# Blocks aligned with batches, their leftovers as a ninth block, and attention between groups of six matmuls

## The chip, the cores and the metric

The kernel runs on one core of a Trainium2 chip. The metric is the device time of one execution in microseconds (us); the time before is the median of three runs. Engines are named as in the profile: PE is TensorE's matmul, PEld its weight load, DVE VectorE, ACT ScalarE, POOL GpSimd, SP SyncE, which here issues every DMA.

## What is computed

```python
# q, k, v: (8 batches, 8 heads, 576 tokens, 64)
scores = q @ k.T / 8
mask_local   = (0 <= rel) & (rel < 32)                  # heads 0 to 3
mask_strided = (0 <= rel) & (pos_k % 32 == pos_q % 32)  # heads 4 to 7
x = softmax(masked scores) @ v        # -> (8, 576, 512), heads side by side
u = x + V.T @ (U.T @ x)               # over tokens; U: 576 x 32, V: 32 x 576
out = u + relu(u @ w_ch1) @ w_ch2     # w_ch1: 512 x 2048, w_ch2: 2048 x 512
```

So each of the 4608 tokens goes through attention inside its batch, a mixing of low rank over the tokens of its batch, and an MLP.

## The kernel before

**The MLP** works on u transposed: features on the partitions, tokens along the free axis, in blocks of `TB` = 512 tokens. 8 x 576 tokens make `NB` = 9 blocks. Every operand is kept as two parts, a rounded one and the remainder (`uh` and `ul`, `gh` and `gl`, two parts of each weight), and a product takes three matmuls. `gemm1(n, fc)` (L413) makes 128 hidden features of block n from four feature chunks: 12 matmuls of 128x128 by 128x512 into `ph`, then ACT (L417) and DVE (L418) make `gh` and `gl`. `gemm2(n, fc)` (L428) adds their part to four accumulators of 512 tokens, again 12 matmuls. There are `NFC` = 16 such chunks fc in a block, and gemm2 runs `LAG` = 2 chunks behind gemm1. `finish(n)` (L431) adds `ul` on DVE (L435) and `uh` on POOL (L436) and stores four tiles `o`. Weights come as 64-bit floats and are converted on chip in 32 chunks (`convert`, ACT L82 and L110, DVE L84 to L87, POOL L111); some in the prefix, the rest in block 0.

**Attention of batch b** is made while block b - 1 runs through the MLP, and that of batch 0 in a prefix (`first_attention`). A pair of heads is a generator (`attention_pair`): loads of kT, qT and vt; scores on PE (mask L143, products L149); maximum and difference on DVE (L157, L158); exponential on ACT (L161); transposes on PE (L170) and a copy on ACT (L173); outputs on PE (L181); normalising on DVE into `x_loc` or `x_str` (L195, L200). Local heads (pairs 0 and 1) always go this way. Strided heads (pairs 2 and 3) do so in batches 0 and 1 (`NSP` = 2). For batches 2 to 7 `strided_heads(b)` makes them with products on POOL (L260, L286) and sums on DVE (L262, L288); their q, k, later v, and their output `o_str[b]` all lie in the one tile `st`, loaded by three DMAs of 576 KB, and at the end ACT copies them into `x_str` (L303, L307).

**Mixing.** `mix_t(b, half)` multiplies x by U on PE (L318, L322) and ends on ACT and DVE in the small tile `tst` (L326 to L335); half 0 is the local heads, half 1 the strided ones. `u_part(b, dc, phase)` then makes u for feature chunk dc: for local heads transposes of x (L389) and a matmul with V (L393) on top of them in PSUM; for strided heads of late batches a matmul (L380) and a DVE add (L382) onto `o_str`. `split` writes `uh` on ACT (L349) and `ul` on DVE or POOL (L350).

**Two phases.** A batch has 576 tokens and a block 512, so batch b fills block b from column 64b on with its first 512 - 64b tokens, and its last 64(b + 1) tokens begin block b + 1. Phase 1 is done in block b - 1, phase 2 in block b (`stretch`). For batches 0 and 1 the strided half of phase 2 waits in the tile `stash`.

**Order.** `stages_of(n)` lists generators with a first and a last chunk; after each gemm1 a `Stage` takes as many steps as put it at its due place. In block n (for b = n + 1, from 2 on) phase 2 of batch n has chunks 2 and 3, the strided heads 4 to 12, the pairs one after the other and local mixing 4 to 10, strided mixing and phase 1 of batch b 13 and 14. The code is then laid out by a scheduler that lists each engine's instructions by priority (the order of the code) and by its own simulated time, and gives out buffers, so neighbours on an engine are not always neighbours in the code.

**Buffers that are shared.** Outside the prefix all small stages (scores, transposes, outputs, mixing, u) take turns in one PSUM tile `px` (`psx2`). In SBUF the tag `att` has `ATT_BUFS` = 7 buffers for kT, qT, s_sb, PT, ta, cv, the strided products tmp and the o tiles. vt and st have one buffer, uh and ul two.

Of the kernel before, what the change touches and what calls it, by code (L numbers as in the profile page):

```python
# [32 lines left out]
def fused_kernel(ctx, tc, lqk, lv, eqk, ev, sqkv, U, V, wts, masks, eye, out):  # L33
# [4 lines left out]
    ap_ = ctx.enter_context(tc.tile_pool(name="ap", bufs=1))  # L38
    ps_acc = ctx.enter_context(tc.tile_pool(name="ps_acc", bufs=2, space=bass.MemoryType.PSUM))
# [77 lines left out]
    stash = ap_.tile([128, 2, 128], F32, name="stash", tag="s_st")  # L117
# [196 lines left out]
    def mix_t(b, half):  # L314
# [9 lines left out]
        yield  # L324
# [4 lines left out]
        yield  # L329
# [6 lines left out]
        yield  # L336

    uT = {}
# [6 lines left out]
    def split(n, dc, cols, src, engine, order=None):  # L345
        uh, ul = (z[:, dc, cols] for z in block_u(n))
        if order is not None:
            uh, ul = uh.rearrange("p (i r) -> p r i", r=32), ul.rearrange("p (i r) -> p r i", r=32)
        nc.scalar.copy(out=uh, in_=src)  # L349
        engine.tensor_tensor(out=ul, in0=src, in1=uh.bitcast(F32), op=ALU.subtract)  # L350

    def stretch(b, phase):
        s0 = TB - 64 * b
        return (b, 0, s0, 64 * b) if phase == 1 else (b + 1, s0, S, 0)

    def u_part(b, dc, phase):
        n, lo, hi, col = stretch(b, phase)
        cols = slice(col, col + hi - lo)
        tst = tsts[b][:, 128 * dc:128 * dc + 128]
        strided = dc >= 2  # L360
        if strided and b < NSP:
            if phase == 2:
                split(n, dc, cols, stash[:, dc - 2, 0:hi - lo], nc.gpsimd)
                return
            px = psx2().rearrange("p a x -> p (a x)")
            for t in range(5):
                w = 128 if t < 4 else 64
                xin = x_str[0:w, t, 128 * dc - 256:128 * dc - 128]
                nc.tensor.matmul(px[:, 128 * t:128 * t + w], xin, ident[0:w, 0:w], is_transpose=True,
                                 start=t in (0, 4), stop=False, skip_group_check=True)  # L370
            nc.tensor.matmul(px[:, 0:512], tst, Vp[:, 0:512], start=False, stop=True, skip_group_check=True)
            nc.tensor.matmul(px[:, 512:576], tst, Vp[:, 512:576], start=False, stop=True, skip_group_check=True)
            src = px[:, 0:S].rearrange("p (r i) -> p r i", i=NCH)
            split(n, dc, cols, src[:, :, 0:hi // 32], nc.vector, True)
            w = S - hi
            nc.scalar.copy(out=stash[:, dc - 2, 0:w].rearrange("p (i r) -> p r i", r=32), in_=src[:, :, hi // 32:NCH])
            return
        if strided:
            px = psx2()[:, 0, 0:hi - lo]
            nc.tensor.matmul(px, tst, Vst[:, lo:hi], start=True, stop=True)  # L380
            src = o_str[b][:, dc - 2, lo:hi]
            nc.vector.tensor_tensor(out=src, in0=px, in1=src, op=ALU.add)  # L382
            split(n, dc, cols, src, nc.gpsimd)
            return
        px = psx2().rearrange("p a x -> p (a x)")
        base, top = lo // 128 * 128, min(S, (hi + 127) // 128 * 128)
        for s in range(base, top, 128):
            w = min(128, top - s)
            nc.tensor.matmul(px[:, s - base:s - base + w], x_loc[0:w, s // 128, 128 * dc:128 * dc + 128], ident[0:w, 0:w],  # L389
                             is_transpose=True, start=(s - base) % 512 == 0, stop=False, skip_group_check=True)  # L390
        for s in range(base, top, 512):
            w = min(512, top - s)
            nc.tensor.matmul(px[:, s - base:s - base + w], tst, Vst[:, s:s + w], start=False, stop=True,  # L393
                             skip_group_check=True)
        split(n, dc, cols, px[:, lo - base:hi - base], nc.vector)

    def u_parts(b, phase, dcs=range(NDC)):
        for dc in dcs:
            u_part(b, dc, phase)
            yield  # L400
# [5 lines left out]
    def gemm1(n, fc):  # L406
# [4 lines left out]
        for dc in range(NDC):  # L411
            for i, (part, ut) in enumerate(((0, uh), (0, ul), (1, uh))):
                nc.tensor.matmul(ph, w_parts[0, g, dc][:, part, fs], ut[:, dc, :],  # L413
                                 start=(dc == 0 and i == 0), stop=(dc == NDC - 1 and i == 2))
        gh = gp.tile([128, TB], F32R, name="gh")
# [3 lines left out]
        return gh, gl  # L419

    def gemm2(n, fc, gh, gl):
# [3 lines left out]
        for m in range(NDC):  # L425
            ms = slice(128 * m, 128 * m + 128)
            for i, (gt, part) in enumerate(((gh, 0), (gl, 0), (gh, 1))):
                nc.tensor.matmul(accs[n][m // 2][:, m % 2], w_parts[1, g, f][:, part, ms], gt,  # L428
                                 start=(fc == 0 and i == 0), stop=(fc == NFC - 1 and i == 2))

    def finish(n):  # L431
        uh, ul = uT[n]
        for m in range(NDC):
            o = att([128, TB], "o")
            nc.vector.tensor_tensor(out=o, in0=accs[n][m // 2][:, m % 2], in1=ul[:, m].bitcast(F32), op=ALU.add)  # L435
            nc.gpsimd.tensor_tensor(out=o, in0=o, in1=uh[:, m].bitcast(F32), op=ALU.add)  # L436
            dma(out=out[m][:, TB * n:TB * n + TB], in_=o)
# [14 lines left out]
    def first_attention():  # L452
# [32 lines left out]
        yield from mix_t(0, 1)  # L485
        yield from mix_t(0, 0)
        for _ in u_parts(0, 1):
            convert(wl["conv"] + 1)
            yield

    def pairs_of(b):
        if b < NSP:
            yield from run_staggered([attention_pair(b, pr) for pr in PAIR_ORDER], 6)
            yield from mix_t(b, 1)
        else:
            yield from attention_pair(b, 0)
            yield from attention_pair(b, 1)
        yield from mix_t(b, 0)

    def rest_of(b):  # L500
        if b >= NSP:
            yield from mix_t(b, 1)
        yield from u_parts(b, 1)

    for _ in first_attention():
        pass
# [7 lines left out]
    class Stage:  # L514
        def __init__(self, gen, start, end, total):
            self.gen, self.start, self.end, self.total, self.done = gen, start, end, total, 0

        def run(self, step):
            if self.gen is None or step < self.start:
                return  # L520
            want = 10 ** 6 if step >= self.end else self.total * (step + 1 - self.start) // (self.end + 1 - self.start)
            while self.done < want:
                self.done += 1
                if next(self.gen, "end") == "end":
                    self.gen = None
                    return

    def stages_of(n):
        b = n + 1
        if b == 1:  # L530
            return [Stage(u_parts(0, 2), 0, 0, 4), Stage(pairs_of(1), 1, 12, 36), Stage(rest_of(1), 13, 14, 4)]
        found = [Stage(u_parts(n, 2), LAG, LAG + 1, 4)] if n < B else []
        if b < B:
            found += [Stage(strided_heads(b), LAG + 2, 12, 82), Stage(pairs_of(b), LAG + 2, 10, 24), Stage(rest_of(b), 13, 14, 7)]
        return found
# [101 lines left out]
```

## Time and profile before

| what | us |
|---|---|
| median of 3 runs (986.08 to 988.97) | 986.51 |
| profiled execution | 990.67 |
| its span in the profile | 988.9 |
| granted clock over the span | 0.958 |
| PE busy / PEld busy | 927.8 / 732.8 |
| DVE / ACT / POOL busy | 541.1 / 252.4 / 414.9 |

Busy times are sums of instruction durations, with overlaps taken once. A matmul's duration contains its fill and drain, so a stream of matmuls looks busy throughout and its price is the distance from start to start. An idle time carries the instruction that released the engine. The granted clock is a share of TensorE's full clock. The views are the page (totals, 40 slices, chain, groups), the stretches (busy time by engine between two times), the timeline, the waits, and the chain of waits.

### The profile page before, as it was taken

How to read it: one execution, taken by the hardware profiler on the slowest of the kernel's cores; microseconds unless marked ns; L12 is line 12 of the kernel's file. 1: busy time of each engine (PE TensorE's matmuls, PEld its weight loads, DVE VectorE, ACT ScalarE, POOL GpSimd, SP SyncE). 2: the span in 40 equal slices, each digit the busy share in tenths (PEclk: the TensorE clock that was granted, in tenths of full speed). 3: DMA queues.
4: the chain of work that ended last, by engine and by line, in shares of the span. 5: the costliest groups of instructions: out<-in, count | busy, mean ns of one | idle time of the engine just before them, and what ended most of it. 6: DMA issues, size and time to landing. Idle time of an engine off the chain costs nothing.

```text
span 988.9 us, 16540 instructions
## 1 busy us (share of the span) xinstructions
PE 927.8 (94%) x6906; PEld 732.8 (74%) x6906; DVE 541.1 (55%) x942; ACT 252.4 (26%) x519; POOL 414.9 (42%) x433
## 2 busy tenths in 40 slices
PE   4689978999999999999999989999899989999996
PEld 2467756687778777888688868887688868888885
DVE  4866475458735883379526982588437941112111
ACT  3454242211421152114221142115211421101010
POOL 1234223586237842488209840784258721002001
PEclk7589988999999999999999999999999999999998
DMA  9932410302012201220110210220122010001001
GB/s 336 408 125 68 140 30 21 115 1 73 26 43 72 74 25 43 72 74 26 43 49 25 74 62 6 73 74 26 43 73 74 1 44 0 1 1 43 1 1 42
DMA packets 22154, 62.40 MB, mean 63 GB/s; under 512 B 2464, under 2 KB 2720, under 8 KB 22080
## 3 DMA queue, kind: packets, MB, share of 16 engines
q1 hardware_dynamic: 22080, 61.36, 17.5%
q8 instruction: 54, 0.88, 0.4%
q14 instruction: 20, 0.16, 0.1%
HBM read 51.91 MB, written 9.44 MB: 62 GB/s over the span
## 4 chain that ended last, share of the span: by engine, by line
PE 67%; issue 10%; POOL 9%; DVE 9%; DMA 3%; ACT 2%; SPq 0%; POOLq 0%; ACTq 0%; DVEq 0%
PE acc L428 31%; PE ph L413 30%; POOL tmp L260 5%; DVE st L288 3%; POOL w L111 3%; DMA st<-in_sqkv_dram 1%; PE px L389 1%; DMA raw<-in_wts_dram 1%; PE px L149 1%; POOL tmp L286 1%; PE px L181 1%; PE px L318 1%; PE px L393 1%; DVE o L435 1%; PE px L170 1%
## 5 line engine op out<-in xcount | busy, mean ns | idle before, releaser
L413 PE MATMUL ph<-uh,w 128*128 128x512 f32 x1152 | 392.7, 401 | 6.7 <-ACT uh L349 5.0
L428 PE MATMUL acc<-gh,w 128*128 128x512 f32 x1152 | 383.9, 395 | 1.5 <-ACT w L110 1.3
L413 PEld LDWEIGHTS ph<-uh,w 128*128 128x128 f32 x1152 | 220.2, 193 | 56.7 <-ACT uh L349 7.8
L428 PEld LDWEIGHTS acc<-gh,w 128*128 128x128 f32 x1152 | 215.9, 189 | 48.4 <-ACT w L110 1.6
L413 PE MATMUL ph<-ul,w 128*128 128x512 f32 x576 | 231.5, 402 | 0.9 <-DVE ul L350 0.5
L428 PE MATMUL acc<-gl,w 128*128 128x512 f32 x576 | 226.2, 393 | 0.0
L418 DVE SCALAR_TENSOR_TENSOR gl<-ph,gh 128x512 fp32r<-128x512 f32 x144 | 98.3, 687 | 211.4 <-ACT gh L417 211.2
L417 ACT ACTIVATE gh<-ph 128x512 fp32r<-128x512 f32 x144 | 85.1, 597 | 419.2 <-PE ph L413 419.0
L260 POOL TENSOR_TENSOR tmp<-st 128x576 f32<-128x576 f32 (+6 forms) x162 | 165.3, 1069 | 32.8 <-DMA st<-in_sqkv_dram 30.1
L436 POOL TENSOR_TENSOR o<-o,uh 128x512 f32<-128x512 f32 x36 | 45.3, 1286 | 282.7 <-DVE o L435 282.7
L286 POOL TENSOR_TENSOR tmp<-st,s_st 128x448 f32<-128x448 f32 (+7 forms) x162 | 134.4, 871 | 31.3 <-DVE s_st L279 26.4
L288 DVE TENSOR_REDUCE st<-tmp 128x64 f32<-128x64 f32 (+8 forms) x162 | 134.8, 884 | 6.2 <-POOL tmp L286 4.8
L413 PEld LDWEIGHTS ph<-ul,w 128*128 128x128 f32 x576 | 111.1, 193 | 25.4 <-DVE ul L350 1.4
L428 PEld LDWEIGHTS acc<-gl,w 128*128 128x128 f32 x576 | 108.4, 188 | 22.6
L262 DVE TENSOR_REDUCE s_st<-tmp 128x9 f32<-128x576 f32 (+6 forms) x162 | 90.4, 572 | 51.5 <-POOL tmp L260 50.7
L111 POOL TENSOR_TENSOR w<-cv,w 128x512 fp32r<-128x512 f32 x32 | 45.2, 1427 | 86.6 <-ACT w L110 86.6
L350 POOL TENSOR_TENSOR ul<-st,uh 128x384 fp32r<-128x384 f32 (+7 forms) x24 | 19.2, 801 | 106.4 <-ACT uh L349 106.4
L303 ACT COPY x_str<-st 32x256 f32<-32x256 f32 x96 | 38.8, 404 | 21.3 <-DVE st L288 20.2
L350 DVE TENSOR_TENSOR ul<-px,uh 128x448 fp32r<-128x448 f32 (+7 forms) x34 | 16.9, 498 | 42.2 <-ACT uh L349 42.1
L382 DVE TENSOR_TENSOR st<-px,st 128x384 f32<-128x384 f32 (+7 forms) x24 | 10.9, 456 | 49.8 <-PE px L380 49.8
L435 DVE TENSOR_TENSOR o<-acc,ul 128x512 f32<-128x512 f32 x36 | 23.1, 686 | 16.8 <-PE acc L428 16.3
L349 ACT CAST uh<-px 128x448 fp32r<-128x448 f32 (+7 forms) x34 | 15.1, 445 | 54.0 <-PE px L393 47.9
(118 smaller groups left out, 534.8 us busy)
## 6 DMA issues: line engine op xcount, KB each, us to landing
raw<-in_wts_dram SPq DMA_DIRECT2D x32, 512.0 KB, 10.2
st<-in_sqkv_dram SPq DMA_DIRECT2D x18, 576.0 KB, 3.9
out_dram<-o SPq DMA_DIRECT2D x36, 256.0 KB, 2.0
vt<-in_lv_dram SPq DMA_DIRECT2D x14, 585.0 KB, 4.1
kT<-in_lqk_dram SPq DMA_DIRECT2D x15, 288.0 KB, 3.9
qT<-in_lqk_dram SPq DMA_DIRECT2D x15, 288.0 KB, 4.1
ve<-in_lv_dram SPq DMA_DIRECT2D x4, 292.5 KB, 6.6
ve<-in_ev_dram SPq DMA_DIRECT2D x4, 292.5 KB, 6.9
```

The lines of the kernel that those rows point to most:

```text
L111: nc.gpsimd.tensor_tensor(out=parts[:, 1], in0=f, in1=parts[:, 0].bitcast(F32), op=ALU.subtract)
L260: nc.gpsimd.tensor_tensor(out=tmp[:, 0:n], in0=sk[:, j0:j0 + n], in1=sq[:, i:i + 1].broadcast_to([128, n, D]), op=ALU.mult)
L262: late.append(lambda tmp=tmp, n=n, i=i, j0=j0: nc.vector.tensor_reduce(out=s_st[:, i, j0:j0 + n], in_=tmp[:, 0:n], axis=AX.X, op=ALU.add))
L286: nc.gpsimd.tensor_tensor(out=tv, in0=sv[:, 0:i + 1, d0:d0 + step], in1=s_st[:, i, 0:i + 1].broadcast_to([128, i + 1, step]), op=ALU.mult)
L288: late.append(lambda tv=tv, i=i, d0=d0, step=step: nc.vector.tensor_reduce(out=sq[:, i, d0:d0 + step], in_=tv.rearrange("p j d -> p d j"), ...
L303: nc.scalar.copy(out=xh[32 * i4:32 * i4 + 32, 0:4], in_=oh[:, i4:16:4])
L350: engine.tensor_tensor(out=ul, in0=src, in1=uh.bitcast(F32), op=ALU.subtract)
L413: nc.tensor.matmul(ph, w_parts[0, g, dc][:, part, fs], ut[:, dc, :], start=(dc == 0 and i == 0), stop=(dc == NDC - 1 and i == 2))
L417: gate[:] = [nc.scalar.activation(out=gh, in_=ph, func=AF.Relu).ins]
L418: nc.vector.scalar_tensor_tensor(out=gl, in0=ph, scalar=0.0, in1=gh.bitcast(F32), op0=ALU.max, op1=ALU.subtract)
L428: nc.tensor.matmul(accs[n][m // 2][:, m % 2], w_parts[1, g, f][:, part, ms], gt, start=(fc == 0 and i == 0), stop=(fc == NFC - 1 and i == 2))
L436: nc.gpsimd.tensor_tensor(out=o, in0=o, in1=uh[:, m].bitcast(F32), op=ALU.add)
```

## The change

- Block b is exactly the first 512 tokens of batch b. The last 64 tokens of each batch are mixed with it (`u_tail`), written as 128 x 4 x 64 values to a tile `rest` in DRAM, and make block 8, which `u_rest` loads during block 7 and splits. Its `finish` adds the loaded u on DVE and has no POOL step. The output is in this order and is put right on the host.
- One phase of mixing per batch. `u_part` becomes `u_local` (two chunks at once), `u_strided` (both chunks), `u_strided_early` for batches 0 and 1, and `u_tail`. The tile `stash` is gone.
- `gemm1` and `gemm2` yield after each six matmuls. A block has 64 such ticks. At each, `tick` gives every task of the block that has reached its start tick and whose predecessors are done its rate of steps.
- For late batches strided heads and pairs begin at tick 0 (the pairs five calls apart, not one after the other), local mixing at 20, local u at 26, strided mixing at 47, strided u and tail at 53. In block 0 pairs begin at tick 2, seven apart, in the order 2, 3, 0, 1; mixing from 30, u from 38.
- Weight conversion in block 0 is paced by tick (0.48 each) instead of two per chunk.

```diff
+    dram = ctx.enter_context(tc.tile_pool(name="dram", bufs=1, space=bass.MemoryType.DRAM))
...
-    stash = ap_.tile([128, 2, 128], F32, name="stash", tag="s_st")
...
+    def u_local(b, dcs):
+        px = psx2()
+        for dc in dcs:
+            ps = px[:, dc % 2]
+            for t in range(4):
+                nc.tensor.matmul(ps[:, 128 * t:128 * t + 128], x_loc[:, t, 128 * dc:128 * dc + 128], ident,
+                                 is_transpose=True, start=t == 0, stop=False, skip_group_check=True)
+            mixed(ps, b, dc, Vst, 0, TB, False)
+        lo, hi = dcs[0] % 2, dcs[-1] % 2 + 1
+        split(b, slice(dcs[0], dcs[-1] + 1), px[:, lo:hi], nc.vector)
+
+    def u_strided(b):
+        px = psx2()
+        for dc in (2, 3):
+            mixed(px[:, dc - 2], b, dc, Vst, 0, TB, True)
+        src = o_str[b][:, :, 0:TB]
+        nc.vector.tensor_tensor(out=src, in0=px, in1=src, op=ALU.add)
+        split(b, slice(2, 4), src, nc.gpsimd)
...
+    def u_tail(b):
+        ps = psx2()[:, 0].rearrange("p (c s) -> p c s", s=64)
+        for dc in range(2):
+            nc.tensor.matmul(ps[:, dc], x_loc[0:64, 4, 128 * dc:128 * dc + 128], ident[0:64, 0:64],
+                             is_transpose=True, start=dc == 0, stop=False, skip_group_check=True)
+        for dc in range(2 if b < NSP else NDC):
+            mixed(ps[:, dc], b, dc, Vst, TB, S, False)
+        tl = tail_of(b)
+        nc.scalar.copy(out=tl[:, 0:2], in_=ps[:, 0:2])
+        if b >= NSP:
+            nc.vector.tensor_tensor(out=tl[:, 2:4], in0=ps[:, 2:4], in1=o_str[b][:, :, TB:S], op=ALU.add)
+        dma(out=rest[:, :, 64 * b:64 * b + 64], in_=tl)
+
+    def u_rest():
+        for dc in range(NDC):
+            last_u[dc] = att([128, TB], "lu")
+            dma(out=last_u[dc], in_=rest[:, dc])
+        for _ in range(8):
+            yield
+        for dc in range(NDC):
+            split(B, dc, last_u[dc], nc.vector)
+            yield
...
+            if n == NB - 1:
+                nc.vector.tensor_tensor(out=o, in0=acc, in1=last_u[m], op=ALU.add)
+            else:
...
+        if b < B:
+            return [
+                task(strided_heads(b), "str", 0, 1.5),
+                task(run_staggered([attention_pair(b, 0), attention_pair(b, 1)], 5), "pairs", 0, 1.0),
+                task(calls(lambda: mix_t(b, 0)), "mix0", 20, 1.0, ("pairs",)),
+                task(calls(lambda: u_local(b, (0, 1))), "u0", 26, 1.0, ("mix0",)),
+                task(calls(lambda: mix_t(b, 1)), "mix1", 47, 1.0, ("str",)),
+                task(calls(lambda: u_strided(b), lambda: None, lambda: None, lambda: u_tail(b)), "u1", 53, 1.0, ("mix1", "u0")),
+            ]
+        if b == B:
+            return [task(u_rest(), "rest", 12)]
...
+            gens = [gemm1(n, fc)]
+            if len(pend) >= LAG:
+                gens.append(gemm2(*pend.pop(0)))
+            for i in range(4):
+                if i // 2 < len(gens):
+                    next(gens[i // 2])
+                tick(n, t, tasks)
+                t += 1
```

More of the change, by code (lines that the diff above doesn't have):

```diff
@@ L356, in u_part @@
[L356 to L384, printed above, removed]
-        px = psx2().rearrange("p a x -> p (a x)")
[L386 to L395, printed above, removed]
@@ L397, in u_parts, with tail_of, mixed @@
-    def u_parts(b, phase, dcs=range(NDC)):
-        for dc in dcs:
-            u_part(b, dc, phase)
+    def tail_of(b):
+        if b not in tails:
+            tails[b] = att([128, NDC, S - TB], "tl")
+        return tails[b]
+    def mixed(ps, b, dc, V, s0, s1, start):
+        nc.tensor.matmul(ps, tsts[b][:, 128 * dc:128 * dc + 128], V[:, s0:s1], start=start, stop=True,
+                         skip_group_check=True)
+    def u_local(b, dcs):
[8 more added lines that the diff above has]
+        split(b, slice(dcs[0], dcs[-1] + 1), px[:, lo:hi], nc.vector)
@@ new lines, in u_strided, with u_strided_early @@
+    def u_strided(b):
[5 more added lines that the diff above has]
+        split(b, slice(2, 4), src, nc.gpsimd)
+    def u_strided_early(b, dc):
+        px = psx2().rearrange("p a x -> p (a x)")
+        for t in range(5):
+            w = 128 if t < 4 else 64
+            xin = x_str[0:w, t, 128 * dc - 256:128 * dc - 128]
+            nc.tensor.matmul(px[:, 128 * t:128 * t + w], xin, ident[0:w, 0:w], is_transpose=True,
+                             start=t in (0, 4), stop=False, skip_group_check=True)
+        mixed(px[:, 0:512], b, dc, Vp, 0, 512, False)
+        mixed(px[:, 512:576], b, dc, Vp, 512, 576, False)
+        src = px[:, 0:S].rearrange("p (r i) -> p r i", i=NCH)
+        split(b, dc, src[:, :, 0:16], nc.vector, "p (i r) -> p r i")
+        nc.scalar.copy(out=tail_of(b)[:, dc].rearrange("p (i r) -> p r i", r=32), in_=src[:, :, 16:NCH])
@@ L484, in first_attention @@
             pass
-        yield from mix_t(0, 1)
-        yield from mix_t(0, 0)
-        for _ in u_parts(0, 1):
+        mix_t(0, 1)
+        mix_t(0, 0)
+        for dc in range(2):
+            u_local(0, (dc,))
             convert(wl["conv"] + 1)
[L489 to L506, printed above, removed]
+        for dc in (2, 3):
+            u_strided_early(0, dc)
+            convert(wl["conv"] + 1)
+    first_attention()
     banks["prefix"] = False
@@ L512, in needed @@
         return 8 * (fc // 4) + 4 + fc % 4
[L514 to L526, printed above, removed]
@@ L528, in stages_of, with task @@
[L528 to L535 removed]
+    done = set()
+    def task(gen, key, start, rate=1.0, after=()):
+        return [gen, key, start, rate, after, 0.0]
@@ new lines, in tick @@
+    def tick(n, t, tasks):
+        if n == 0:
+            load_weights(c0 + 8 + 3 * (t + 4) // 4)
+            convert(max(int(c0 + 0.48 * (t + 3)), needed(min(t // 4 + 1, NFC - 1))))
+        for k in list(tasks):
+            gen, key, start, rate, after, credit = k
+            if t < start or not done.issuperset(after):
+                continue
+            k[5] += rate
+            while k[5] >= 1.0:
+                k[5] -= 1.0
+                if next(gen, "end") == "end":
+                    done.add(key)
+                    tasks.remove(k)
+                    break
@@ L537, in fused_kernel @@
     for n in range(NB):
-        stages = stages_of(n)
+        tasks, t = plan(n), 0
+        done.clear()
         for fc in range(NFC):
```

68 lines of the change are left out of this document (40 added, 28 removed).

## The prediction

> **What bounds the kernel now.** I read the page first, for the busiest engine, its clock and the chain of work that ended last.
>
> ```profile
> span 988.9 us, 16540 instructions
> PE 927.8 (94%) x6906; PEld 732.8 (74%) x6906; DVE 541.1 (55%) x942; ACT 252.4 (26%) x519; POOL 414.9 (42%) x433
> ...
> PEclk7589988999999999999999999999999999999998
> ...
> PE acc L428 31%; PE ph L413 30%; POOL tmp L260 5%; DVE st L288 3%; POOL w L111 3%; DMA st<-in_sqkv_dram 1%; PE px L389 1%; DMA raw<-in_wts_dram 1%; PE px L149 1%; POOL tmp L286 1%; PE px L181 1%; PE px L318 1%; PE px L393 1%; DVE o L435 1%; PE px L170 1%
> ```
>
> TensorE's two MLP lines carry most of the chain; what is left is POOL and DVE work of the strided heads, DMAs of that stage, and waits. "Busy" at 94% says little, since a pipelined matmul counts its drain. So the price of a matmul comes from the chain of waits, where twelve MLP matmuls run undisturbed:
>
> ```profile
> 856.09 2.72 PE ph L413 x12
> ```
>
> That is 2.72/12 = 0.227 us for one. The code has 9 blocks x 16 chunks x 24 = 3456, which makes 783 us; a block's 384 take 87.0. The other 206 us of the span are what a change can reach. To place them I cut the span into stretches that begin with each block's first L413 matmul (columns: length, busy time and count of PE, PEld, DVE, ACT, POOL, granted clock, DMA share, GB/s):
>
> ```profile
> 0.00:51.30 51.30, 25.68 (x653) 17.03 (x653) 33.97 (x75) 20.76 (x36) 8.81 (x13) 0.67 0.99 374
> 51.30:177.90 126.60, 114.44 (x1037) 88.12 (x1038) 79.52 (x142) 48.81 (x89) 39.17 (x30) 0.90 0.20 69
> 177.90:282.10 104.20, 102.62 (x745) 80.22 (x744) 63.94 (x111) 28.25 (x61) 56.38 (x62) 0.98 0.15 51
> 282.10:384.40 102.30, 100.06 (x737) 79.18 (x737) 65.29 (x114) 26.49 (x59) 58.44 (x63) 1.00 0.15 52
> 384.40:486.80 102.40, 101.21 (x741) 79.49 (x739) 66.58 (x114) 26.56 (x59) 59.80 (x65) 1.00 0.15 52
> 486.80:591.70 104.90, 100.96 (x736) 79.93 (x736) 67.75 (x116) 26.50 (x59) 61.84 (x66) 0.98 0.16 56
> 591.70:696.90 105.20, 102.40 (x737) 81.27 (x737) 66.75 (x114) 26.48 (x59) 58.36 (x64) 0.97 0.15 51
> 696.90:801.60 104.70, 100.86 (x736) 79.96 (x736) 66.61 (x115) 26.54 (x60) 58.07 (x63) 0.98 0.13 45
> 801.60:888.50 86.90, 86.89 (x380) 71.20 (x381) 14.53 (x24) 12.46 (x23) 4.10 (x5) 0.98 0.02 7
> 888.50:988.90 100.40, 92.71 (x410) 76.42 (x408) 16.13 (x24) 9.57 (x16) 9.96 (x8) 0.98 0.06 21
> ```
>
> A prefix of 51.3; block 0 with 126.6; six blocks that carry a strided batch each, 623.7 together; blocks 7 and 8, 187.3. No helper engine fills a stretch (DVE at most 68 of 105, POOL 62), so a middle block loses its 17 us over 87 to attention's own matmuls and to order. The order shows at a boundary, in the timeline of PE (start, length, last bracket: idle before and its releaser):
>
> ```profile
> 587.70 0.64 PE L318 MATMUL px<-x_str,U_sb 128*32 128x256 f32 x8
> 588.16 0.29 PE L322 MATMUL px<-x_str,U_sb 128*32 128x64 f32 x8
> 590.60 0.41 PE L389 MATMUL px<-ident,x_loc 128*128 128x128 f32 x2 [2.15 <-DVE ta L328]
> ...
> 591.72 1.22 PE L413 MATMUL ph<-uh,w 128*128 128x512 f32 x2 [0.59 <-ACT uh L349]
> ```
>
> and, over all such boundaries, in PE's waits (us in total, times, longest):
>
> ```profile
> PE px L389 <- DVE ta L328: 6.5, 3, 2.2
> ```
>
> Mixing is the last thing before the boundary. PE runs dry behind it for 2.15, then 0.59 us, and the stretch that follows is granted 0.97 of the clock, while the stretches from 282.1 and 384.4, which are not among the three with this wait, have 1.00. Why mixing is late stands in the DMA queue's waits and in the timelines of POOL and DVE:
>
> ```profile
> SPq L57 <- POOL ul L350: 98.9, 6, 26.9
> ...
> 624.64 1.99 POOL L260 TENSOR_TENSOR tmp<-st 128x64 f32<-128x64 f32 x4 [5.18 <-DMA st<-in_sqkv_dram]
> ...
> 684.66 1.38 DVE L295 STREAM_TRANSPOSE st<-st 128x1152 f32<-128x1152 f32 x1
> ```
>
> Six times the load of the next strided batch waits for the POOL split of the previous batch's leftover tokens, which runs in the next block. POOL begins 33 us after the boundary at 591.7 and the strided chain ends at 686, 61 us later and 11 before the next boundary; mixing and four u tiles must fit in those 11.
>
> **The change part by part.** The sum is made against the profiled run's span.
>
> *Middle blocks.* With every split of batch b inside one block, st is free at tick 53 to 57 of 64, and the plan starts the strided stage at tick 0. From the rows just shown the chain needs 61 us; begun some 6 us into the block (a load of 5.2 before it) it ends near 67, and the plan's own pace (74 calls at 1.5 a tick, a tick being 87.0/64 = 1.4 us and some attention) ends near 75. Some 20 us are left where 11 were. So the dry spells at the boundary go, and what is late next is PE's own work:
>
> ```profile
> 622.56 0.45 PE L143 MATMUL px<-masks_sb 128*128 128x320 bf16 x2
> 632.47 0.92 PE L149 MATMUL px<-kT,qT 64*32 64x32 f32 x72
> 640.93 0.80 PE L170 MATMUL px<-ident,s_sb 128*128 128x128 f32 x5
> 648.93 0.98 PE L181 MATMUL px<-vt,PT 64*32 64x65 f32 x72
> ...
> 598.85 0.76 PE L389 MATMUL px<-ident,x_loc 128*128 128x128 f32 x4
> 599.53 0.47 PE L393 MATMUL px<-Vst,tst 96*128 96x448 f32 x1
> ...
> 611.31 0.34 PE L380 MATMUL px<-Vst,tst 96*128 96x384 f32 x1
> ```
>
> One pair is 0.45+0.92+0.80+0.98 = 3.15 (the overlap of each with its successor is kept in, as the price of changing over), two are 6.3. Mixing is two halves of 0.75 (from 587.70 to 588.45), 1.5, unchanged. Local u: two times four transposes and one wide matmul, 2 x 1.23 = 2.5. Strided u: two matmuls of 512, 0.34 x 512/384 = 0.45 each, 0.9. The tail has two transposes of 64 rows and four matmuls of 64 columns, which no row shows: between 0.29 (eight matmuls of 64 columns, L322) and 1.23 (a whole local u); I take 0.6, as it is nearer to the former. With 87.0 that makes 98.8. Waits that stay: at worst 3.5 (the two best stretches, 102.3, less 98.8), at best none; I take 1.2, a third, because what still waits there is mostly one boundary. So 100.0 a block, 600 for six against 623.7: **23.7 gained**, which includes the clock that PE loses at the boundaries ((1-0.98) x 104 to (1-0.97) x 105, about 2 to 3 us in four of the six).
>
> About that clock. The Trainium skill, "TensorE: Matmul & The Clock Gate", section "What's actually happening", lets the clock fall only after a whole idle window of about 3.4 us. By this the waits of 2.15 us would not be what costs the clock here, and it would not come back: the sum would be 11 us higher, the rival below. The rows side with the waits so far, since the stretch behind the 2.15 us wait is among those with a lower clock and the best two have none.
>
> *Block 0.* Its PE list is 87.0, four pairs 12.6, mixing 1.5, local u 2.5, two early strided u (five transposes 0.95, wide matmuls about 0.65) 3.2, two tails 1.2: 108.0. The clock costs (1-0.90) x 126.6 = 12.7 now; the page's third digit (0.8 of 24.7 us) puts up to 5 of that into the start, which nothing touches, and I keep 4. The waits of PE in this stretch:
>
> ```profile
> PE px L318 <- DVE x_loc L195: 4.7, 1, 4.7
> PE px L170 <- ACT s_sb L161: 1.9, 1, 1.9
> ...
> PE ph L413 <- ACT w L110: 1.5, 1, 1.5
> ```
>
> All sit at the end of a dependency chain of batch 1 that is drawn out over 12 chunks; the new plan begins it two ticks earlier, runs it at 1.0 instead of 0.75 calls a tick, and spaces the weight conversions per tick. DVE's 79.5 us of work stay, now denser beside the pairs, so I keep 7 of such waits (ends: 0 and 13). 108+4+7 = 119 against 126.6: **7.6 gained**.
>
> *Blocks 7 and 8.* Batch 7's leftovers no longer pass through PE in block 7, which holds MLP only. The end of the kernel, in the timeline:
>
> ```profile
> 980.12 2.48 DVE L435 TENSOR_TENSOR o<-acc,ul 128x512 f32<-128x512 f32 x4 [5.71 <-PE acc L428]
> ...
> 980.82 0.39 PE L428 MATMUL acc<-gh,w 128*128 128x512 f32 x1
> 980.94 4.92 POOL L436 TENSOR_TENSOR o<-o,uh 128x512 f32<-128x512 f32 x4 [76.78 <-DVE o L435]
> ```
>
> Now 7.7 us pass from the last matmul (981.2) to the span's end: POOL until 985.86, then 3.0 of DMA. For the ninth block the POOL add is gone, so it is DVE until 982.60 and the same 3.0: 4.4. With 174.1 for the matmuls and 1 for a wait on the accumulators (the four lu tiles hold four of seven shared buffers, so block 7's four o tiles queue for three): 179.5 against 187.3, **7.8 gained**.
>
> *At nothing.* The trip through DRAM: eight stores of 128 KB and four loads of 256 KB. The nearest rows (last number: us to landing):
>
> ```profile
> raw<-in_wts_dram SPq DMA_DIRECT2D x32, 512.0 KB, 10.2
> ...
> out_dram<-o SPq DMA_DIRECT2D x36, 256.0 KB, 2.0
> ```
>
> Between the last store (end of block 6) and the first use (tick 20 of block 7) lie over 25 us of matmuls. Without that cover it would cost a store and a load, once: 4 to 20. On SP's queue the store waits for the tail's DVE add; behind it stand the next st loads, which need that add anyway. The longer split (1024 elements at once on ACT and DVE or POOL) has 15 us of cover. The prefix keeps its work: 51.3.
>
> Sum: 51.3 + 119 + 600 + 179.5 = **950**. The run around the profile took 990.67, 1.8 over its span, and lies 4.2 over the median of 986.51, so a median is the span less 2.4: 947.6.
>
> **The rivals.**
> *No wait left.* The 15 us of waits that I keep (7.2+7+1) go too: 935, median 932. For it: DVE and POOL are below two thirds in every middle stretch. Against: one PSUM buffer serves all small stages.
> *The clock stays lower.* If the clock falls for another reason than the waits, about 11 us ((1-clock) x length of the stretches from 177.9 to 888.5) stay: 961, median 959.
> *Order is made elsewhere.* L149 at 632.47 runs inside a group of L413, where the code puts attention only between groups; a simulated timeline already places it. If the new start ticks change little, only removed work and the end are gained: 7.8, and some 7 in the other seven blocks (eight u pieces a batch, each with its own matmul and split, become four; near 1 us a block, an estimate): 974, median 972. Against: the SP waits above are real dependencies that the change removes.
> *Slower: the accumulators are released late.* finish runs at tick 7. Until now nothing else is active there; now strided products, kT, qT and s_sb hold the same seven buffers, POOL's queue holds products ahead of the o adds, and on SP's the stores of o may stand behind the second pair's vt, which has one buffer and waits for the first pair's outputs:
>
> ```profile
> L260 POOL TENSOR_TENSOR tmp<-st 128x576 f32<-128x576 f32 (+6 forms) x162 | 165.3, 1069 | 32.8 <-DMA st<-in_sqkv_dram 30.1
> ...
> SPq L57 <- PE px L181: 268.2, 14, 26.1
> ```
>
> A product before an add costs 1.1, the vt two ticks at most. An o tile holds one through DVE 0.62, POOL 1.23 and a DMA of 3.0, 4.9 us. With one buffer free the fourth add starts 14.7 us later, where gemm2's second half needs it within 4: PE stands some 11 us, at half clock for 2 more, at six boundaries: 78, so 1028, median 1026. It outweighs the gain from 6.5 us a boundary; with two buffers free the delay is about 2 us and the change still gains.
> *No change*: the edits cancel, 986.
>
> **How the numbers follow.** Forecast 0.56; no wait left 0.12; clock stays 0.08; order elsewhere 0.12; late accumulators 0.08; no change 0.04. Time: 948. The range 930 to 975 takes in the first four, 0.88, with 2 us about their ends. Faster by over 0.3% (3 us, about what a measurement of this kernel can tell from no change) 0.88, within 0.04, slower 0.08.
>
> **What would show it.** Right: L260 starts within 10 us of a block's first L413 matmul; x_str is mixed 15 us or more before the boundary; no PE wait over 1 us there; stretches of 98 to 101 with a clock of 0.99 or 1.00; block 7 free of px; about 4.4 us from the last matmul to the end. Wrong: the L260 chain stretching past 85 us, PE waits before the first acc matmul of a block released by the o adds, or block 0 still over 124.

## The result and the profile after

The kernel takes 957.07 us, the median of three runs (956.82 to 957.07), against 987.74 us (four runs, 986.08 to 989.01) for the kernel before beside it: a ratio of 0.969, 95% interval 0.9666 to 0.9713. The forecast was 948.0, range 930 to 975. One execution of the new kernel, the profiled one, took 2239.97 us and is left out; so the trace of after shown here is that of another execution of the same kernel, first of the experiments below, which took 958.38 us.

The page of after, its totals and the clock in 40 slices:

```profile
span 956.6 us, 16502 instructions
PE 915.5 (96%) x6896; PEld 726.5 (76%) x6896; DVE 528.3 (55%) x911; ACT 247.2 (26%) x486; POOL 402.9 (42%) x407
...
PEclk8589997999999999999999999999999999999999
...
```

Beside the page of before, the span loses 32.3 us. PE's idle time gives 20.0 of it (61.1 to 41.1, span less busy), its busy time 12.3 (927.8 to 915.5); the latter holds both time at half clock and a shorter list of matmuls. Behind the seventh slice the clock row holds nothing but nines. The stretches that begin with each block's first gemm1 matmul (columns: length, busy time and count of PE, PEld, DVE, ACT, POOL, granted clock, DMA share, GB/s) say where:

```profile
0.00:48.30 48.30, 25.56 (x653) 17.05 (x653) 31.09 (x71) 19.02 (x33) 7.77 (x13) 0.69 0.98 374
48.30:179.50 131.20, 118.17 (x1041) 89.12 (x1042) 81.36 (x151) 52.78 (x94) 43.86 (x36) 0.89 0.26 89
179.50:276.20 96.70, 96.70 (x726) 77.07 (x725) 62.43 (x101) 25.80 (x54) 51.95 (x52) 1.00 0.14 44
276.20:375.00 98.80, 98.80 (x737) 78.80 (x736) 63.93 (x108) 25.81 (x54) 57.71 (x60) 1.00 0.17 55
...
473.90:573.60 99.70, 99.16 (x737) 78.94 (x736) 65.10 (x108) 25.33 (x54) 57.66 (x61) 1.00 0.17 55
...
771.20:859.20 88.00, 88.00 (x391) 72.64 (x391) 16.26 (x25) 12.65 (x22) 7.45 (x5) 1.00 0.09 26
859.20:956.60 97.40, 92.66 (x409) 76.39 (x407) 16.12 (x24) 9.57 (x16) 5.08 (x4) 1.00 0.06 22
```

| stretch | before | forecast | after |
|---|---|---|---|
| prefix | 51.3 | 51.3 | 48.3 |
| block 0 | 126.6 | 119 | 131.2 |
| blocks 1 to 6 | 623.7 | 600 | 591.7 |
| blocks 7 and 8 | 187.3 | 179.5 | 185.4 |

The middle blocks gained more than was forecast, block 0 became longer instead of shorter. In a middle block PE's busy time is now the stretch itself, 98.80 of 98.80 at a clock of 1.00: the matmul list is the bound. Some of PE's waits of after, over the whole run (us in total, times, longest):

```profile
PE px L170 <- ACT s_sb L161: 4.4, 2, 2.5
...
PE acc L446 <- ACT gh L434: 4.1, 2, 2.2
PE ph L428 <- ACT w L111: 3.4, 3, 2.1
...
PE px L383 <- DVE ta L327: 1.4, 1, 1.4
```

L446 is gemm2 here, L428 gemm1, L383 the transposes of the early strided u. They lie in block 0, but for 1.9 of the first row's 4.4, which lies in the prefix. From block 1 on, PE's waits come to 0.5 us in all, and none in the run names an add of `finish`.

How the strided stage now lies, by POOL's first product of two batches, DVE's last transpose of the stage and the end of strided mixing on PE, from the timelines of after:

```profile
284.87 1.99 POOL L260 TENSOR_TENSOR tmp<-st 128x64 f32<-128x64 f32 x4 [8.90 <-DMA st<-in_sqkv_dram]
384.32 7.55 POOL L260 TENSOR_TENSOR tmp<-st 128x64 f32<-128x64 f32 x9 [9.09 <-DMA st<-in_sqkv_dram]
...
360.93 1.38 DVE L295 STREAM_TRANSPOSE st<-st 128x1152 f32<-128x1152 f32 x1
...
362.11 0.32 PE L322 MATMUL px<-x_str,U_sb 128*32 128x64 f32 x8
```

POOL begins 8.7 us into the block at 276.2 (33 before). From first product to end of the transpose the stage takes 77 us, not 61; the pairs now run beside it, which is probably why. It still ends 13 us before the boundary at 375.0.

The trip through DRAM, by the tile `rest` (last row: from issue to landing, min, median, max):

```profile
L58 SPq DMA_DIRECT2D rest<-tl x8: 524/525/597, 60.6 to 776.8; - x8
L58 SPq DMA_DIRECT2D lu<-rest x4: 320/352/424, 779.1 to 786.3; - x4
...
DMA to landing us min/median/max: 2.2/2.4/5.2
```

The last load is issued at 786.3, the block that uses it begins at 859.2. The split in between, on ACT, waits 1.9 us for that load.

### The profile page after: what moved, and what is told of

Same layout as the page of the kernel before. It is cut to its first block, busy times and chain, and to the rows that moved or that the text cites. A ratio compares the mean times of both kernels' runs of the same rounds, so it can differ in the third digit from the quotient of the medians.

```text
span 2238.2 us, 16502 instructions
## 1 busy us (share of the span) xinstructions
PE 2207.4 (99%) x6896; PEld 1291.8 (58%) x6896; DVE 525.2 (23%) x911; ACT 247.1 (11%) x486; POOL 402.7 (18%) x407
## 4 chain that ended last, share of the span: by engine, by line
PE 97%; DVE 1%; DMA 1%; ACT 0%; issue 0%; SPq 0%; DVEq 0%; ACTq 0%
PE ph L428 45%; PE acc L446 45%; PE px L181 1%; PE px L356 1%; PE px L149 1%; PE px L170 1%; PE px L364 1%; PE px L318 1%; DMA raw<-in_wts_dram 1%; PE px L143 1%; DMA ve<-in_ev_dram 0%; DVE cv L88 0%; PE px L322 0%; DVE cv L86 0%; DVE cv L85 0%
## 5 line engine op out<-in xcount | busy, mean ns | idle before, releaser
L428 PE MATMUL ph<-uh,w 128*128 128x512 f32 x1152 | 844.7, 818 | 3.0 <-ACT w L111 2.4
L446 PE MATMUL acc<-gh,w 128*128 128x512 f32 x1152 | 831.7, 809 | 2.2 <-ACT gh L434 2.2
L446 PEld LDWEIGHTS acc<-gh,w 128*128 128x128 f32 x1152 | 393.8, 343 | 266.4 <-issue 257.9
L428 PEld LDWEIGHTS ph<-uh,w 128*128 128x128 f32 x1152 | 394.1, 344 | 264.1 <-issue 247.8
L446 PE MATMUL acc<-gl,w 128*128 128x512 f32 x576 | 469.4, 815 | 0.0
L428 PE MATMUL ph<-ul,w 128*128 128x512 f32 x576 | 467.1, 811 | 0.0
L435 DVE SCALAR_TENSOR_TENSOR gl<-ph,gh 128x512 fp32r<-128x512 f32 x144 | 99.3, 690 | 1102.0 <-ACT gh L434 1101.7
L446 PEld LDWEIGHTS acc<-gl,w 128*128 128x128 f32 x576 | 197.7, 343 | 134.5 <-issue 132.7
L428 PEld LDWEIGHTS ph<-ul,w 128*128 128x128 f32 x576 | 197.8, 343 | 128.4 <-issue 125.4
L260 POOL TENSOR_TENSOR tmp<-st 128x576 f32<-128x576 f32 (+6 forms) x162 | 165.6, 1047 | 486.5 <-DVE s_st L262 107.5
L262 DVE TENSOR_REDUCE s_st<-tmp 128x9 f32<-128x576 f32 (+6 forms) x162 | 86.1, 564 | 30.9 <-POOL tmp L260 30.9
L327 DVE TENSOR_TENSOR ta<-px,ta 32x256 f32<-32x256 f32 x42 | 17.6, 420 | 78.8 <-ACT ta L325 77.9
L170 PE MATMUL px<-ident,s_sb 128*128 128x128 f32 (+1 forms) x95 | 30.2, 471 | 4.2 <-ACT s_sb L161 4.2
```

Of the source, the lines that this page charges most:

```text
L170: nc.tensor.transpose(out=pp[:, 128 * t:128 * t + n], in_=s_sb[0:n, t].rearrange("p h x -> p (h x)"), identity=ident[0:n, 0:n])
L260: nc.gpsimd.tensor_tensor(out=tmp[:, 0:n], in0=sk[:, j0:j0 + n], in1=sq[:, i:i + 1].broadcast_to([128, n, D]), op=ALU.mult)
L262: late.append(lambda tmp=tmp, n=n, i=i, j0=j0: nc.vector.tensor_reduce(out=s_st[:, i, j0:j0 + n], in_=tmp[:, 0:n], axis=AX.X, op=ALU.add))
L435: nc.vector.scalar_tensor_tensor(out=gl, in0=ph, scalar=0.0, in1=gh.bitcast(F32), op0=ALU.max, op1=ALU.subtract)
```

## The experiments

Each is an edit of the new kernel, but for the third, which edits the kernel before. The ratio is to the kernel before on the same chip, in brackets its 95% interval.

**Why do the middle blocks gain?** One theory: because the tile `st` is released at the end of the batch's own block, whatever the start ticks are. Its rivals: because of the early start ticks; because of the groups of six; because a batch is now mixed in one phase and not in two, which leaves PE less to do and fewer turns in `px`.

*a_again*: the new kernel, unchanged.

> The changed kernel once more, for the stretches of its profile. By the prediction: prefix 51, block 0 about 119, six middle blocks of about 100, blocks 7 and 8 together 179.5; the measured median of 957.07 is 9 us above the forecast, so one of these terms should be about 9 us larger. If the clock rival holds, the middle stretches show 0.97 to 0.98 of the clock; if late accumulators do, PE waits before the first acc matmul of a block on the o adds.

958.38 us, with the profile above.

*e1_twelve*: both ticks of a gemm come after its twelve matmuls.

```diff
-            for i in range(4):
-                if i // 2 < len(gens):
-                    next(gens[i // 2])
-                tick(n, t, tasks)
-                t += 1
+            for i in range(2):
+                if i < len(gens):
+                    next(gens[i])
+                    next(gens[i])
+                for _ in range(2):
+                    tick(n, t, tasks)
+                    t += 1
```

> The changed kernel with the groups of six undone: both ticks of a gemm come after its twelve matmuls. Main theory (the start ticks and the freed st buffer make the gain; the scheduler places the small matmuls by itself anyway): at most 3 us slower than the changed kernel, 955 to 960. Rival (the finer grain makes the gain): about 1 to 3 us lost in each of seven blocks, 965 to 977.

957.7 us, ratio 0.9709 (0.9679 to 0.9739). A middle block of this kernel, in the stretches:

```profile
374.18:472.99 98.81, 98.81 (x737) 78.81 (x736) 63.73 (x108) 25.67 (x54) 57.79 (x60) 1.00 0.17 55
```

The grain does nothing that can be measured.

*e2_late*: the start ticks of the late batches are moved back, and their rates fitted to that.

```diff
-                task(strided_heads(b), "str", 0, 1.5),
-                task(run_staggered([attention_pair(b, 0), attention_pair(b, 1)], 5), "pairs", 0, 1.0),
-                task(calls(lambda: mix_t(b, 0)), "mix0", 20, 1.0, ("pairs",)),
-                task(calls(lambda: u_local(b, (0, 1))), "u0", 26, 1.0, ("mix0",)),
+                task(strided_heads(b), "str", 16, 2.06),
+                task(run_staggered([attention_pair(b, 0), attention_pair(b, 1)], 12), "pairs", 16, 0.86),
+                task(calls(lambda: mix_t(b, 0)), "mix0", 44, 1.0, ("pairs",)),
+                task(calls(lambda: u_local(b, (0, 1))), "u0", 52, 1.0, ("mix0",)),
```

> The changed kernel with the stages of the six middle blocks begun as late as before: strided heads and pairs at tick 16, local mixing at 44, local u at 52. Main theory (the early start of the strided stage makes the middle blocks shorter): the 61 us of that stage end some 89 us into the block, mixing and u fall on the boundary again, and four to six us come back in each of six blocks: 980 to 992. Rival (the gain is the removed second phase, not the time of the start): 957 to 964.

955.04 us, ratio 0.9674 (0.9645 to 0.9704): nothing is lost, so the expectation's main theory is refuted. The timeline of POOL and DVE, and a stretch, in this kernel:

```profile
291.17 15.18 POOL L260 TENSOR_TENSOR tmp<-st 128x64 f32<-128x64 f32 x17 [4.71 <-DMA st<-in_sqkv_dram]
...
355.10 1.38 DVE L295 STREAM_TRANSPOSE st<-st 128x1152 f32<-128x1152 f32 x1
```

```profile
373.20:471.70 98.50, 98.50 (x738) 79.00 (x737) 63.97 (x108) 25.43 (x54) 57.79 (x60) 1.00 0.17 55
```

The block before this one began at 274.63. POOL starts 16.5 us into it, 8 later than in after, and the stage then takes 65 us instead of 77 and ends earlier within its block (81.9 us in, against 86.1). So the start ticks are not the reason, and the 77 us of after are slack that nobody needs.

*e3_before_early*: the kernel before, with its two phases, but with the early start.

```diff
-        found = [Stage(u_parts(n, 2), LAG, LAG + 1, 4)] if n < B else []
+        found = [Stage(u_parts(n, 2), LAG, LAG, 4)] if n < B else []
...
-            found += [Stage(strided_heads(b), LAG + 2, 12, 82), Stage(pairs_of(b), LAG + 2, 10, 24), Stage(rest_of(b), 13, 14, 7)]
+            found += [Stage(strided_heads(b), LAG, 11, 82), Stage(pairs_of(b), 0, 6, 24), Stage(rest_of(b), 12, 14, 7)]
```

> The kernel before with its stages begun as early as its two phases allow: phase 2 wholly in chunk 2, the strided heads from chunk 2 instead of 4, the pairs from chunk 0, phase 1 from chunk 12. Main theory: the strided stage begins some 11 us earlier, the waits at the boundaries shrink by half or more, 2 to 4 us in each of six blocks: 964 to 976. Rival (only blocks aligned with batches bring it, since phase 2 stays on PE's path at the head of each block): 983 to 990.

1017.64 us, ratio 1.0311 (1.028 to 1.0342): slower, which neither expectation had. A stretch, POOL's first product in it, and PE's waits in this kernel (block start 387.6):

```profile
387.60:497.00 109.40, 102.72 (x737) 80.73 (x737) 65.36 (x113) 26.52 (x59) 58.94 (x63) 0.97 0.15 48
```

```profile
431.37 14.37 POOL L260 TENSOR_TENSOR tmp<-st 128x64 f32<-128x64 f32 x16 [5.60 <-DMA st<-in_sqkv_dram]
```

```profile
PE px L389 <- DVE ta L328: 11.6, 5, 3.7
PE px L322 <- ACT x_str L307: 11.4, 9, 2.4
```

The early ticks made the stage start later, 43.8 us into the block instead of 33: the last split of the leftovers, which releases `st`, ends 38 us into the block (POOL L350, at 425.8) instead of 28 or less, probably since it now shares `px` with the pairs; that was not tried alone. PE's wait for `ta` at the boundaries grew from 6.5 us to 11.6, and 11.4 us more are spent before L322. Without an earlier release the early ticks give nothing here.

*e5_hold* and *e8_hold2*: in the new kernel the release alone is taken back. The strided columns of the tail stay in `st` until a copy in the next block, at tick 17 in the first and 12 in the second, where the copy has a tile of its own. The diff is that of the first.

```diff
-            nc.vector.tensor_tensor(out=tl[:, 2:4], in0=ps[:, 2:4], in1=o_str[b][:, :, TB:S], op=ALU.add)
+            src = o_str[b][:, :, TB:S]
+            nc.vector.tensor_tensor(out=src, in0=ps[:, 2:4], in1=src, op=ALU.add)
+            dma(out=rest[:, 0:2, 64 * b:64 * b + 64], in_=tl[:, 0:2])
+            return
...
+    def tail_hold(b):
+        t2 = att([128, 2, S - TB], "tl")
+        with tc.issue_after(gate[0]):
+            nc.scalar.copy(out=t2, in_=o_str[b][:, :, TB:S])
+        dma(out=rest[:, 2:4, 64 * b:64 * b + 64], in_=t2)
...
-            return [
-                task(strided_heads(b), "str", 0, 1.5),
+            held = [task(calls(lambda: tail_hold(b - 1)), "hold", 17)] if b > NSP else []
+            return held + [
+                task(strided_heads(b), "str", 17, 1.9, ("hold",) if held else ()),
...
```

> The changed kernel with st held into the next block as before: the strided columns of the tail stay in st, and an ACT copy of them (behind the relu of chunk 3 or 4 of the next block) and its store release st; the strided heads follow from tick 17. Late starts alone cost nothing, since the scheduler starts a ready stage ahead of its tick (POOL still began 16 us into a block); here the start is late by a dependency. Theory (the release of st sets the start, some 61 us of strided work follow, and mixing falls on the boundary): POOL begins 30 to 36 us into a block, and 3 to 6 us are lost in each of five blocks: 970 to 988. Rival (the second phase's own PE, DVE and px work at the head of the block made the waits, not the held tile): within 4 us of the changed kernel, 954 to 961.

1034.49 us, ratio 1.0485 (1.0456 to 1.0513). POOL starts 59 us into its block (272.7), much later than intended, and the time lies outside both expected ranges. The stage, a stretch and PE's waits:

```profile
332.02 9.21 POOL L260 TENSOR_TENSOR tmp<-st 128x64 f32<-128x64 f32 x11 [26.91 <-DMA st<-in_sqkv_dram]
```

```profile
381.20:493.70 112.50, 103.83 (x738) 81.47 (x737) 65.19 (x109) 26.09 (x55) 57.90 (x61) 0.92 0.15 48
```

```profile
PE px L356 <- DVE tst L333: 17.8, 7, 2.9
PE px L322 <- ACT x_str L307: 10.9, 7, 2.1
PE px L318 <- ACT x_str L303: 10.4, 5, 2.1
```

> As e5_hold, where POOL began 59 to 64 us into a block and each middle block took 108 to 113, but held for less: from tick 12, with the copy in a tile of its own instead of one of the seven shared buffers. POOL should begin 28 to 36 us into a block, as it did before the change. Theory (the time at which st comes free sets a middle block's length): 101 to 106 a block as before the change, 968 to 988 in all. Rival (e5_hold lost its time to the buffer that it held and to vt queued behind, not to the late start): within 4 us of the changed kernel, 954 to 961.

988.07 us, ratio 1.001 (0.9997 to 1.0023): with this delay the whole gain is gone. POOL's products of one batch, PE's longest group of waits, and a stretch, in this kernel (block start 273.84):

```profile
306.58 2.00 POOL L260 TENSOR_TENSOR tmp<-st 128x64 f32<-128x64 f32 x4 [3.67 <-DMA st<-in_sqkv_dram]
311.91 0.89 POOL L260 TENSOR_TENSOR tmp<-st 128x320 f32<-128x320 f32 x1 [3.34 <-PE px L181]
319.13 24.92 POOL L260 TENSOR_TENSOR tmp<-st 128x384 f32<-128x384 f32 x22 [6.33 <-issue]
```

```profile
PE px L394 <- DVE st L375: 7.9, 6, 1.3
...
PE ph L437 <- POOL ul L348: 7.4, 6, 1.7
```

```profile
378.30:481.80 103.50, 100.83 (x738) 79.78 (x737) 65.19 (x109) 25.90 (x56) 57.94 (x60) 0.98 0.17 53
```

POOL starts 32.7 us into the block, as in the kernel before, and block length and clock are those of before too. The kernels can be read as one loop through the single tile `st`: the stage, and the turnaround from the end of the L295 transpose to the next batch's first product (mixing, strided u, the release, the next load). From the starts and ends of L260 and L295:

| kernel | turnaround | stage | sum | block |
|---|---|---|---|---|
| before (blocks from 696.9) | 43.7 | 61.0 | 104.7 | 104.7 |
| after | 22.0 | 77.3 | 99.3 | 98.9 |
| e2_late | 33.0 | 65.5 | 98.5 | 98.5 |
| e8_hold2 | 28.1 | 75.4 | 103.5 | 103.5 |
| e3_before_early | 47.5 | 62.3 | 109.8 | 109.4 |
| e5_hold | 49.8 | 62.7 | 112.5 | 112.5 |

The sum must equal the block in steady state; what the table shows is the split. In after and e2_late PE's list of 98.5 to 98.8 sets the block and the stage has slack: with the shortest turnaround and stage seen the loop would close in 22.0 + 61.0 = 83 us (an estimate). In the other four, by this reading, the loop sets it and PE waits.

How late a release may be also depends on the stage. With the shortest one, 61.0, a turnaround over 98.8 - 61.0 = 37.8 must cost time; before, e3 and e5 lie above that. e8_hold2 does not: its turnaround of 28.1 is shorter than the 33.0 of e2_late, which loses nothing, and with e2_late's stage it would close in 93.6 (an estimate). So its loss needs the stage of 75.4 as well. That is probably due to the buffers that products and pairs share (POOL waits 3.34 us there for the pairs' outputs, and 6.33 for something that the profile does not name). A held release with late pairs was not tried.

Nor is the loop the whole gain. In before the stage began 13.5, 19.7 and 26.5 us into the blocks from 177.9, 282.1 and 384.4 and ended 23, 22 and 14 us ahead of their ends, so the loop had not closed yet. These three blocks took 308.9 us even so, against 294.4 for the first three of after: 14.5 of the 32 us that the six gained, of which 2.0 are nine MLP matmuls that after runs elsewhere. Among what after lacks there is the second phase, with its matmuls and its waits. The experiments show that the gain is lost when the release is held back; what one phase of mixing is worth by itself, no run separates.

**Why did block 0 become longer?** One theory: the weight conversions, which queue on ACT in the order of the code behind the latest relu. The rival: the seven buffers of `att`.

*e4_scratch*: three of the four pairs of batch 1 get kT and qT from the scratch tiles of the prefix.

```diff
-            kT, qT = att([128, S], "kT"), att([128, S], "qT")
+            kT, qT = kq or (att([128, S], "kT"), att([128, S], "qT"))
...
-                task(run_staggered([attention_pair(1, pr) for pr in (2, 3, 0, 1)], 7), "pairs", 2, 1.0),
+                task(run_staggered([attention_pair(1, pr, kq=scr_kq(k)) for k, pr in enumerate((2, 3, 0, 1))], 7), "pairs", 2, 1.0),
```

> The changed kernel with kT and qT of three of batch 1's four pairs in the prefix's scratch tiles instead of the seven shared buffers. Block 0 took 131 us where 119 were forecast. Theory A (prefetched kT and qT hold up to four of the seven buffers for 20 us and starve the weight conversions, which need one each): block 0 falls by 5 to 12 us, 945 to 952. Theory B (DVE's and ACT's own queues in the plan's order make the conversions late): within 2 us of the changed kernel, 955 to 959.

956.88 us, ratio 0.9698 (0.9664 to 0.9732), block 0 130.1 us against 131.2: the buffers are not it.

*e6_fast*: conversions are laid out faster.

```diff
-            convert(max(int(c0 + 0.48 * (t + 3)), needed(min(t // 4 + 1, NFC - 1))))
+            convert(max(int(c0 + 0.64 * (t + 3)), needed(min(t // 4 + 1, NFC - 1))))
```

> The changed kernel with the conversions of block 0 paced at 0.64 instead of 0.48 a tick. In block 0 ACT's queue holds the exponential of batch 1's third pair ahead of the next conversions and waits 9 us for it, and PE then waits for weights. Theory (conversions stand too late in the queues): moved ahead they are done before the pairs block ACT, block 0 falls from 131 to 119 to 126, and the kernel takes 946 to 953. Rival (the total of ACT's and DVE's work, or the pairs' chain itself, sets block 0): 955 to 960.

954.6 us, ratio 0.9672 (0.9649 to 0.9696), block 0 129.1: a small part.

*e7_nogate*: a conversion's first step on ACT need not be issued behind the latest relu.

```diff
-            f = to_f32(raws[c], 128, 512, True)
+            f = to_f32(raws[c], 128, 512)
```

> The changed kernel without the order between a conversion's first step on ACT and the last relu before it in the code. Theory that this order makes the conversions late: 947 to 953. Rival (it binds nothing, the scheduler's own order has them in the same places): within 2 us of the changed kernel, 955 to 959. It may also be worse, if conversions now stand ahead of a relu that PE needs: 960 to 966.

951.28 us, ratio 0.9643 (0.9615 to 0.9671). Its block 0, and a middle block, in the stretches:

```profile
47.20:170.70 123.50, 113.27 (x1041) 85.78 (x1042) 85.67 (x151) 52.73 (x93) 45.01 (x36) 0.94 0.28 99
...
366.20:465.20 99.00, 99.00 (x738) 78.95 (x737) 64.17 (x108) 25.24 (x54) 57.73 (x61) 1.00 0.17 55
```

Of the edits tried alone it is the one that matters: block 0 falls from 131.2 to 123.5 and its clock rises from 0.89 to 0.94, and the middle blocks stay.

**The best version.** *e9_late_nogate* joins e2_late and e7_nogate; *e10_all* adds e4_scratch; *e11_pace* is e9_late_nogate with 0.56 in place of 0.48 conversions a tick.

> The late ticks of e2_late and the free conversions of e7_nogate together. If their gains (2 and 6 us) have separate causes, middle blocks and block 0, they add up: 947 to 951. If one took the other's place: 951 to 955.

> e9_late_nogate with the scratch tiles of e4_scratch for batch 1's kT and qT. With conversions freer, buffers could now bind: 943 to 947. If they don't, as in e4_scratch: within 2 us of e9_late_nogate, 947 to 951.

> e9_late_nogate with conversions at 0.56 instead of 0.48 a tick. If block 0 still waits for weights that stand too late in the queues: 944 to 948. If the pairs' chain binds now, as in e6_fast, where the waits moved to the boundary: 948 to 953.

948.69 us (0.9603, 0.9581 to 0.9625), 948.25 (0.9605, 0.9583 to 0.9628) and 951.11 (0.9641, 0.9617 to 0.9666). The first two cannot be told apart and beat both kernels; the buffers do not bind here either, and more conversions per tick did not help with the order on ACT free. By their stretches block 0 takes 126.4, 124.4 and 127.7 in them, more than the 123.5 of e7_nogate, though what they add to it concerns later blocks or proved idle; why was not tried.

## Why the prediction was right, and where it was not

**Right: the middle blocks and their mechanism.** The release moved, the boundary waits of 2.15 and 0.59 us went, the clock came back to 1.00. The list worked out at 98.8 is what five of the six blocks measure (98.8 to 99.7; the first, 96.7, has nine MLP matmuls fewer). That it fits to the tenth is luck: in the block from 375.0, each matmul taken from its start to the next one's, the MLP takes 89.1 (87.0 in the sum), the pairs 5.5 (6.3), mixing 1.6 (1.5), u and tail together 2.5 (4.0). The 1.2 of kept waits did not come. Two reasons given beside it were wrong. "The plan starts the strided stage at tick 0" was no part of the gain (e2_late); and the chain ended at 86 us, not near 67 or 75, since it had slack and, probably, shared its buffers with the pairs. So the sign in the list that x_str is mixed 15 us before the boundary was missed, with 13, at no cost.

**The step that failed: block 0, "7.6 gained".** It lost 4.6. PE has nearly as many instructions in it as before (1041 and 1037, of them 15 MLP matmuls fewer by the counts of their lines), so what failed are the 4 kept for the clock and the 7 for waits: 1 - 0.89 of 131.2 us is 14.4 for the clock alone, and PE stands idle for 131.2 - 118.2 = 13.0. With the list of 108.0 less 3.4 for the 15 matmuls that makes 132.0, near the 131.2 measured. A block 0 over 124 was among the forecast's own signs of being wrong. The forecast named denser DVE work and set it aside with "I keep 7", and took the pacing of the conversions as a help. The timelines of DVE, ACT and POOL in after show one stall of the kind:

```profile
109.53 0.82 DVE L157 TENSOR_REDUCE mx<-px 128x10 f32<-128x640 f32 x1 [5.42 <-PE px L149]
...
111.13 0.42 DVE L85 TENSOR_SCALAR cv<-cv 128x512 int32<-128x512 int32 x1
...
111.25 0.74 ACT L161 ACTIVATE s_sb<-s_sb 128x640 f32<-128x640 f32 x1 [9.14 <-DVE s_sb L158]
...
113.79 1.28 POOL L112 TENSOR_TENSOR w<-cv,w 128x512 fp32r<-128x512 f32 x1 [10.59 <-ACT w L111]
```

PE comes to the scores of a pair at 108.58. DVE stands 5.42 us before their maximum and ACT 9.14 before their exponential; the next conversion steps stand behind them in both queues (on DVE from 111.13), POOL stands for 10.59, and PE then waits for `w` and `gh`. But this stall is not what e7_nogate took away. ACT's waits for the exponentials in block 0, in before, after and e7_nogate:

```profile
ACT s_sb L161 <- DVE s_sb L158: 13.0, 3, 6.5
...
ACT s_sb L161 <- DVE s_sb L158: 13.3, 3, 9.1
...
ACT s_sb L161 <- DVE s_sb L158: 16.5, 3, 8.5
```

They are longest in the kernel with the shortest block 0, and POOL's conversions have a gap of 11.12 us in before and 11.37 in e7_nogate too. What e7_nogate shows is that the conversions' place behind the relu costs some 5 us of the kernel (957.07 to 951.28 is 5.8, by the two ratios it is 4.6). In its block 0 the clock's loss falls from 14.4 us to 7.4 (0.06 of 123.5), PE's idle time from 13.0 to 10.2, so most of it is half clock. Which wait brought that clock down is not shown. Block 0 also holds all of batch 1's early strided u, a part of which lay in block 1 before. How the 12.2 us divide beyond that stays open: 123.5 us is still above the 119 forecast.

**Blocks 7 and 8.** 185.4 against 179.5 is a matter of where the boundary falls: by the counts of the two MLP lines, 793 matmuls lie in these blocks (768 before), 25 x 0.227 = 5.7 us that earlier blocks shed; like for like it is 179.7. The end of after, from the chain of waits (PE) and the timelines of DVE and SP:

```profile
943.70 8.17 PE acc L446 x36
...
950.82 2.48 DVE L460 TENSOR_TENSOR o<-acc,lu 128x512 f32<-128x512 f32 x4 [5.76 <-PE acc L446]
951.54 2.13 SPq L58 DMA_DIRECT2D out_dram<-o  x4
```

From the last matmul at 951.9 it is 4.7 us to the end, for 4.4 forecast and 7.7 before. The cover of the trip through DRAM was there, with some 70 us before the block that uses it. The prefix came out 3.0 shorter, which no step foresaw and no run explains.

**The total.** Prefix -3.0, block 0 +12.2, middle -8.3, end +5.9: 6.8 over the parts. So the middle's surplus hides most of block 0's miss in the sum. The rest of the 9 us by which the median exceeds 948 is, but for rounding, the distance from span to median: it was taken as 2.4 below the span, and is 0.5 above the span of the execution shown.

**The rivals.** That the clock stays low for another reason is refuted: 1.00 wherever the waits are gone, 0.92 to 0.98 where e3, e5 and e8 bring them back. "No wait left" held in the middle blocks alone. Late accumulators did not show. "Order is made elsewhere" was half right: the late ticks of e2_late cost nothing, so readiness counts more than ticks, but the change moves readiness: with the release held back the gain is gone.

## What to carry to other kernels

Where a scheduler places work by readiness, look for the buffer whose release closes a loop from one block to the next, and compare stage plus turnaround with the bound engine's list; here the release had to move, and the start ticks did not matter. Once the loop is shorter than the list, further shortening gives nothing (8 us of later start cost nothing; a held release, with the start 24 us later, cost all 31). A shorter list also pays in blocks where no such loop is closed. In a stretch where pairs and conversions share the queues of ACT and DVE, price the order in the queues and not the engines' busy shares.

## What the runs showed of the hardware

PE's clock can fall behind stretches that are far from idle. Four stretches of 3.4 us behind the boundary at 378.3 in e8_hold2, PE alone (length, PE busy, clock, DMA share, GB/s):

```profile
386.20:389.60 3.40, 2.14 (x10) 1.00 0.00 0
389.60:393.00 3.40, 2.16 (x16) 1.00 0.25 38
393.00:396.40 3.40, 3.23 (x64) 0.50 0.41 155
396.40:399.80 3.40, 3.40 (x45) 1.00 0.02 5
```

PE is busy for 2.14 and 2.16 of 3.40 us, its waits in that experiment's rows above are 1.7 at the longest, and the next 3.4 us run at 0.50. From 180 us on and up to the last matmuls, the traces of before, e3, e5 and e8 hold 23 falls of the clock: the 3.4 us ahead of a fall are busy for a share of 0.15 to 0.63, and all such windows without a fall for 0.55 or more, all but five of them for 0.66 or more (worked out from PE's records, on the grid of 3.413 us that the clock's records lie on). No sharp limit comes out of this, since the two groups overlap. The Trainium skill, "TensorE: Matmul & The Clock Gate", "What's actually happening", asks for a whole idle window of about 3.4 us. The window length agrees with the lengths here, which are 3.4 us or multiples; the condition, read as a window without work, does not. So the forecast was right to side with the waits.
